# Later loads of the attention stacks, fewer transfers of x, and an earlier split of v's weights in a kernel of attention and a gated MLP

## The chip, the cores and the metric

The kernel runs on one core of a Trainium2 chip. A core has five engines that work side by side, each through its own list of instructions in order: TensorE (PE, matrix products; PEld is its loading of weights), VectorE (DVE), ScalarE (ACT), GpSimd (POOL) and SyncE (SP), which here only issues transfers. Sixteen DMA engines move data between the chip's large memory (DRAM) and the core's on-chip memory. The metric is the device time of one execution in microseconds (us). The kernel before took 2613.21 us (median of three executions, 2612.97 to 2613.29).

## The reference

`x` has 2048 tokens of 576 features; attention has 32 heads of 18 features, the MLP 4608 hidden units. All is fp32.

```python
xn = _layernorm(x)                                   # over the 576 features, eps 1e-5
q, k, v = split(xn @ wqkv)                           # 32 heads x 18
p  = softmax(einsum("bhqd,bhkd->bhqk", q, k) * 18 ** -0.5)
s  = (p @ v) @ wo
h  = (xn @ w_gate) * (xn @ w_up)                     # 576 -> 4608
g  = silu(h @ w_down)                                # 4608 -> 576
return x + s * g
```

## The kernel before, in words

**Numbers in two parts.** TensorE multiplies in a reduced form of fp32. An operand that must keep its precision is therefore held as two parts, a high one (a copy by ACT that rounds) and a low one (the difference, by DVE or POOL). A product is then three matmuls: high by high, low by high, high by low.

**Three stages.** In the *prologue* (0 to 197 us of the trace) x is normalised, turned so that features lie on partitions, and multiplied by the weights of q, k and v, chunk by chunk; a chunk is 512 tokens and there are four. q and k are stored, in their two parts, to the DRAM array `sqk` (lines 440 to 455), v to `sv` (`v_block`), the turned x to `sx`. The *main stage* (197 to about 2530 us) does attention's scores and the MLP mixed with each other. In the *epilogue* (to 2610 us) attention's output is multiplied by `wo` and everything is joined.

**The prologue's place.** v's weights come in two halves of 288 columns. `v_split(h)` splits half `h` into parts: five pieces, each an ACT copy (L493) and a POOL difference (L494), into `wv`. `v_block` multiplies the x of 128 tokens by `wv` (L502), first half 0, then half 1. In the loop over chunks `c` and blocks `b`, the step `norm` starts the layernorm of chunk `c + 2`; its ACT part is a tiny square root, `rs` (L344), that waits for statistics of DVE.

**The main stage's two array halves.** TensorE's array is used as two halves, each with 64 rows: partitions 0 to 63 (r = 0) and 64 to 127 (r = 1). Half 0 does the first look at each head's scores: 64 *a items*, each a matmul 128 queries x 512 keys (L648) whose maximum DVE takes (L650). When a head is through, its maxima are folded (L656), negated and split (L662, L666), turned and written by SP as two more rows (`mr`, L686) under the head's q. Half 1 does the same scores again, transposed and with the maximum subtracted by these rows: 64 *b items* (L700), each followed by ACT's exponential (L702) into `pt`. The *visits* multiply `pt` by v (L711); there are three for a head, of 6, 5 and 5 tiles of keys, before the change and after it.

The MLP's units run between the items: for each of 18 units of a chunk, 27 matmuls for up on half 0 and 27 for gate on half 1 (L753), then down (L804). At a unit's gate end the hidden value is `us` times the gate (L766), and its high part is made by ACT (`hs`, L771), its low part by POOL (`hs`, L784, in `low_now`). Down's results are summed into `acc` by DVE (L867) or by ACT and POOL. Weights of the MLP are split in chunk 0, kept in DRAM, and read back in the later chunks, one 1152 KB transfer for a unit's gate or up (`wgu`, L244) and one for its down (`wd`, L283).

**The stacks.** Both kinds of items read q and k from two tiles. Each holds in 18-row bands the high or low part of one head, so that the three products come out of one matmul. A head's *whole* tile is loaded in three transfers of 18 rows x 2048 tokens (144 KB each), its *turning* tile in two halves, part 0 and part 1, of three transfers of 18 x 1024 each (72 KB each). Both come from `sqk` by `load_stack` (L314 to L319), on SP. There are two whole tiles (they alternate by head) and one turning tile for each half of the array, whose halves are written over while the head runs. `stack_turn(r, h, i, h0)` is called at each item `i` of head `h` and says from which item a load may go (`at`: its old contents have been read) and at which item it must go (`by`):

```python
for at, by, g, part in ((0, 48, h + 1, None), (32, 48, h + 1, 0), (0, 16, h, 1)):
```

From `at` on, the load waits in the list `stacks`. Each gate end takes the first from it (`high`, L769 to L776); what is still there at item `by` is loaded at once.

**What sets the order.** A planner (`order()`) writes the instructions of the main stage while it simulates the engines with fixed costs: it keeps a clock for each half of the array (`clk`), times at which engines and banks come free, and for the transfers of SP one queue, at a rate of 0.24 MB per us:

```python
def moved(start, size):
    queue[0] = max(queue[0], start) + size / 0.24
    return queue[0] + 2.0
```

`moved(done - 0.4, 1.18)` books a weight load at each gate end (`done` is when the gate's last product has been taken), about 1.1 us ahead of the moment at which `high` runs. The planner lets a matmul of the MLP go only when its weights or its x are there by this booking (`loaded`, `downed`, `there`). On the chip SP works through its list in order.

**x for the next chunk.** At the last unit of a chunk, as soon as one of the nine blocks of x (64 features each, the high and the low part of 512 tokens) has been used for the last time, `x_block` loads the same block of the next chunk from `sx` over it, for each half its own copy: half 0 by SP, half 1 by POOL's own queue (L465 for block 4, which is in two parts, L468 for the others). A block is 64 partitions x 1024 numbers, 256 KB. In POOL's list these issues stand among its differences.

Of the kernel before, what the change touches and what calls it, by code (L numbers as in the profile page):

```python
# [20 lines left out]
FT = mybir.dt.float32  # L21
# [20 lines left out]
def kernel(  # L42
# [31 lines left out]
    sx = dram.tile([NCH, 9, 64, 2, 512], FT, name="sx")  # L74
# [101 lines left out]
    def engine(eng, start, length):  # L176
        start = max(free[eng], start)
        free[eng] = start + max(length - HIDDEN[eng], 0.03)
        return start + length
# [134 lines left out]
    def load_stack(r, h, part):  # L314
        tile, kind = (whole[h % 2], r == 0) if part is None else (turning, r != 0)
        cs = slice(0, S) if part is None else slice(part * S // 2, (part + 1) * S // 2)
        rows = slice(h * DH, (h + 1) * DH)
        for i, low in enumerate((0, 0, 1) if kind else (0, 1, 0)):
            nc.sync.dma_start(tile[r + i * DH:r + (i + 1) * DH, cs].bitcast(FT), sqk[int(kind), low, rows, cs])  # L319
# [120 lines left out]
    def qk_block(b, c):  # L440
        w, ninth = (t[:, b % 2] for t in wq[b // 2])
        p = bank("a" if nqk[0] % 2 else "b", 2)
        nqk[0] += 1
        for n, (a, e) in enumerate(QK_PAIRS):
            nc.tensor.matmul(p, w[:, a, :] if a < 9 else ninth, xcs[c][:, e, :], start=n == 0,  # L445
                             stop=n == len(QK_PAIRS) - 1)
        hl = pp.tile([128, 2, 512], FR, name="hl", bufs=3)
        nc.scalar.activation(hl[:, 0, :], p, AF.Copy)
        nc.vector.tensor_tensor(hl[:, 1, :], p, hl[:, 0, :].bitcast(FT), op=OP.subtract)
        g0 = blocks[b]  # L450
        for kind in range(2):
            lo, hi = max(g0, kind * D), min(g0 + 128, (kind + 1) * D)
            if lo < hi:
                dst = sqk[kind, :, lo - kind * D:hi - kind * D, c * 512:(c + 1) * 512]
                nc.sync.dma_start(dst.rearrange("h r s -> r h s"), hl[lo - g0:hi - g0].bitcast(FT))


    def x_part(b, part):
        return divmod(2 * b + part, 9)

    def x_block(c, b, r):
        queue = nc.gpsimd if r else nc.sync
        if b == 4:
            for part in range(2):
                queue.dma_start(xg[part][r:r + 64, 8 - 8 * part, :].bitcast(FT), sx[c, b, :, part, :])  # L465
        else:
            i, k = x_part(b, 0)
            queue.dma_start(xg[i][r:r + 64, k:k + 2, :].bitcast(FT), sx[c, b])  # L468

    vbox, vrows, vturn = {}, [], [0]  # L470

# [14 lines left out]
    def v_split(h):  # L486
        if h == 0:
            vbox["w"] = vp.tile([128, 10, D], FR, name="wv")
            more_rows(vp, 3)
        raw, wv = vbox["raw"], vbox["w"]  # L490
        cs = slice(h * HALF, (h + 1) * HALF)
        for k, d, lo in ((0, 0, 4), (1, 1, 5), (2, 2, 6), (3, 3, 7), (4, 8, 9)):
            nc.scalar.activation(wv[:, d, cs], raw[:, k, :], AF.Copy)  # L493
            nc.gpsimd.tensor_tensor(wv[:, lo, cs], raw[:, k, :], wv[:, d, cs].bitcast(FT),  # L494
                                    op=OP.subtract)
# [50 lines left out]
    for c in range(NCH):  # L546
        if c + 2 < NCH:
            load_x(c + 2)
        for b in range(3):
            qk_block(b, c)  # L550
            if c == 0 and b == 0:
                w_now(2)
        if c + 1 < NCH:
            to_columns(c + 1)
        for b in range(3, 6):
            qk_block(b, c)
            if b < 5 and c + 2 < NCH:
                norm(c + 2, (0, 1) if b == 3 else (2, 3))
            if c in (1, 2):
                x_store(c, range(3 * (b - 3), 3 * (b - 2)))  # L560
            if c < 2 and b == 3:
                v_split(c)
            if c == 0 and b == 5:
                v_fetch(1)
            if c == NCH - 1 and b == 3:
                w_now(3)
        if c == 1:
            w_fetch(3)
            for t in range(4):
                v_block(t)  # L570
            w_fetch(4)
        if c == 2:
            w_now(4)
# [56 lines left out]
    with ExitStack() as mid:  # L630
# [130 lines left out]
        def gate_end(n, ps):  # L761
            u, j = divmod(n, 2)
            if j == 0:
                hs[u] = mp.tile([128, 2, 2, 512], FR, name="hs", bufs=2)
            h32 = us.pop(n)
            nc.vector.tensor_tensor(h32, ps, h32, op=OP.mult)  # L766
            g_get(n + 2)
            hj = hs[u][:, j]

            def high(end):  # L770
                nc.scalar.activation(hj[:, 0, :], h32, AF.Copy)  # L771
                lows.append((n, hj, h32))
                pool_later.append((end + 0.1, 1.30, low_now))
                if stacks:
                    load_stack(*stacks.pop(0))
                    moved(end + 1.4, 0.88)  # L776

            return high

# [169 lines left out]
        def stream(r, kind):  # L949

            def glu(n):
                c, q = units[n // 2]
                box = []
                for k in range(len(TERMS)):
                    def work(k=k):
                        if k == 0:
                            box.append(gu_start(r, n))
                        gu_op(r, n, box[0], k)
                        if q == NF2 - 1 and n % 2 and k % 3 == 2 and c < NCH - 1:
                            x_block(c + 1, k // 3, 64 * r)  # L960
                            if r:
                                there["x", c + 1, k // 3, r] = engine("POOL", clk[r] + 0.5, 0.75 + 0.6 * (k == 14)) + 3.0
                            else:
                                there["x", c + 1, k // 3, r] = moved(clk[r] + 0.5, 0.285)
                        if n == 2 * len(units) - 1 and k == 13:
                            xdone.append(r)
                            if len(xdone) == 2:
                                wo_fetch()
                        if k == len(TERMS) - 1:
                            highs.append((gate_end if r else up_end)(n, box[0]))  # L970
                    end = (("DVE", 0.685) if r else ("ACT", 0.595)) if k == len(TERMS) - 1 else None
                    yield 0.231, k == 0, work, end, ("g", n, k), len(TERMS)

            def down(u, n):
                own = alone(u, n)
                key = u, n, r * own
                s, i = divmod(n, 2)
                for k in range(len(DTERMS)):
                    def work(k=k):
                        if (own or r == 0) and k == 0:  # L980
                            passed[key] = down_start(r, u)
                        down_op(r, u, s, i, passed[key], k, {"POOL": nc.gpsimd, "ACT": nc.scalar, "DVE": nc.vector}[soonest()])
                        if (own or r) and k == len(DTERMS) - 1:
                            acts.append(by_act(u, i, clk[r] + 0.33))
                            down_end(u, s, i, passed.pop(key), acts[-1])
                    end = None
                    if (own or r) and k == len(DTERMS) - 1:
                        end = (None, 0.0)
                    yield 0.132, (own or r == 0) and k == 0, work, end, ("d", u, 6 * n + k), len(DTERMS)

            if kind == "g":
                for n in range(2 * len(units)):
                    yield from glu(n)
            else:
                for u in range(len(units)):
                    for n in range(8):
                        yield from down(u, n)
# [19 lines left out]
# [4 lines that stand above are left out]
# [31 lines left out]

        def stack_turn(r, h, i, h0):

            for at, by, g, part in ((0, 48, h + 1, None), (32, 48, h + 1, 0), (0, 16, h, 1)):
                if not (g < H and (g > h0 if part is None else g > 0)):
                    continue
                if i == at:
                    stacks.append((r, g, part))
                if i == by and (r, g, part) in stacks:  # L1060
                    stacks.remove((r, g, part))
                    load_stack(r, g, part)
# [381 lines left out]
```

## Time and profile before

| what | us |
|---|---|
| median of three executions | 2613.21 |
| the profiled execution | 2611.95 |
| its span (first to last instruction) | 2610.2 |
| TensorE busy | 2595.7 (99%) |
| VectorE busy | 1795.3 (69%) |
| ScalarE busy | 1564.0 (60%) |
| GpSimd busy | 691.1 (26%) |

A row of a timeline is: start, length, engine, line, operation, output <- input, tile, count, and in brackets the idle time just before and what ended it. Some rows join several instructions (`x25`). A row of the list of waits is: engine, tile and line of the waiting instruction, what it waited for, us in total, times, longest. A row of the windows is: from:to, length, the busy time (and number) of PE, PEld, DVE, ACT and POOL, TensorE's granted clock, the busy share of the DMA engines, and GB/s; for one line of the kernel, only the busy time of its engine. A row of a group gives the busy time in total, the mean in ns, and the idle time before with its causes. The page lists transfers with their size and, where it can be told, the median time from issue to landing.

### The profile page before, as it was taken

To read this page: it belongs to the slowest core of one execution; us is meant where nothing else is said; L and a number is where in the kernel's file an instruction comes from. 1 tells how busy PE (TensorE), PEld (TensorE's weight loads), DVE (VectorE), ACT (ScalarE), POOL (GpSimd) and SP (SyncE) were. 2 spreads that over 40 slices of the span, in tenths; PEclk is the share of its full clock that TensorE was granted. 3 is DMA by queue.
4 is the path that set the end of the run, shared out by engine and by line. 5 is a ranking of instruction groups with operands and counts; after the bars stand their busy time and mean duration, and the time that the engine had idled before them with its cause. 6 is when DMAs were issued, how large, how long until landed. Compare 5 with 4: busy or idle time off the path is not lost.

```text
span 2610.2 us, 59616 instructions
## 1 busy us (share of the span) xinstructions
PE 2595.7 (99%) x24504; PEld 2130.0 (82%) x24504; DVE 1795.3 (69%) x2985; ACT 1564.0 (60%) x3119; POOL 691.1 (26%) x731
## 2 busy tenths in 40 slices
PE   8999999999999999999999999999999999999999
PEld 7899878777878877887778888778788778777789
DVE  7208677677777877777777777777777777777436
ACT  4223667676766666666656666666666566666742
POOL 3114545343421222222121222112121222112115
PEclk9999999999999999999999999999999999999999
DMA  7799767667573534554463445344564444343356
GB/s 239 236 293 260 205 189 207 177 194 198 173 189 114 167 129 144 175 159 149 144 174 124 139 158 151 121 135 137 146 174 130 142 142 148 128 136 109 110 200 214
DMA packets 206928, 434.34 MB, mean 166 GB/s; under 512 B 82976, under 2 KB 132800, under 8 KB 176448
## 3 DMA queue, kind: packets, MB, share of 16 engines
q1 hardware_dynamic: 202288, 415.48, 52.6%
q0 software_dynamic: 4368, 15.04, 2.0%
q8 instruction: 193, 3.16, 0.5%
q14 instruction: 79, 0.65, 0.1%
HBM read 314.64 MB, written 110.56 MB: 163 GB/s over the span
## 4 chain that ended last, share of the span: by engine, by line
PE 96%; DMA 2%; DVE 1%; SPq 1%; ACT 0%; issue 0%; POOL 0%; ACTq 0%; DVEq 0%
PE pg L753 35%; PE pg L711 17%; PE pg L804 16%; PE pa L648 11%; PE pb L700 9%; PE pg L1396 2%; PE pg L502 1%; PE pb L445 1%; PE pa L445 1%; DMA sqk<-hl 1%; SPq L534 1%; DVE st L342 0%; DMA draw<-in_B_w_down_dram 0%; DMA sv<-vo 0%; PE pb L1373 0%; DVE mx L650 0%
## 5 line engine op out<-in xcount | busy, mean ns | idle before, releaser
L650 DVE TENSOR_REDUCE mx<-pa 128x1 f32<-128x512 f32 x2016 | 1345.6, 686 | 318.8 <-PE pa L648 182.7
L702 ACT ACTIVATE pt<-pb 128x512 f32<-128x512 f32 x2004 | 1148.7, 601 | 525.8 <-PE pb L700 384.8
L753 PE MATMUL pg<-xc,wgu 64*128 64x512 f32 x7776 | 1391.9, 391 | 0.1
L753 PEld LDWEIGHTS pg<-xc,wgu 64*128 64x128 f32 x7776 | 1053.7, 186 | 55.9 <-issue 0.8
L804 PE MATMUL pg<-wd,hs 64*128 64x288 f32 x6816 | 827.0, 293 | 0.7 <-DVE acc L867 0.7
L804 PEld LDWEIGHTS pg<-wd,hs 64*128 64x128 f32 x6816 | 773.9, 185 | 11.8 <-DVE acc L867 0.9
L648 PE MATMUL pa<-whole,turning 54*128 54x512 f32 x1999 | 783.5, 398 | 0.0
L700 PE MATMUL pb<-whole,turning 56*128 56x512 f32 x1987 | 778.5, 399 | 0.0
L711 PE MATMUL pg<-pt,vt 128*32 128x512 f32 x4096 | 459.3, 594 | 0.9 <-DVE acc L867 0.8
L784 POOL TENSOR_TENSOR hs<-us,hs 128x512 fp32r<-128x512 f32 x144 | 186.2, 1293 | 894.7 <-ACT hs L771 718.0
L648 PEld LDWEIGHTS pa<-whole,turning 54*128 54x128 f32 x1999 | 363.8, 184 | 71.8 <-issue 60.5
L700 PEld LDWEIGHTS pb<-whole,turning 56*128 56x128 f32 x1987 | 361.3, 185 | 7.0
L831 POOL TENSOR_TENSOR acc<-acc,st 128x288 f32<-128x288 f32 x288 | 231.7, 808 | 505.2 <-ACT st L861 289.4
L711 PEld LDWEIGHTS pg<-pt,vt 128*32 128x32 f32 x4096 | 123.3, 110 | 277.3 <-issue 269.0
L717 DVE TENSOR_TENSOR oc<-oc,pg 128x512 f32<-128x512 f32 x64 | 44.0, 687 | 287.9 <-PE pg L711 287.9
L254 POOL TENSOR_TENSOR wgu<-wraw,wgu 128x384 fp32r<-128x384 f32 x108 | 108.0, 1016 | 194.8 <-ACT wgu L253 108.8
L861 ACT ACTIVATE st<-pg 128x288 f32<-128x288 f32 x288 | 118.8, 413 | 31.3 <-PE pg L804 21.3
L867 DVE TENSOR_TENSOR acc<-acc,pg 128x288 f32<-128x288 f32 x257 | 114.6, 448 | 29.5 <-PE pg L804 24.1
L766 DVE TENSOR_TENSOR us<-pg,us 128x512 f32<-128x512 f32 x144 | 98.5, 684 | 31.4 <-PE pg L753 26.3
L759 ACT ACTIVATE us<-pg 128x512 f32<-128x512 f32 x144 | 86.2, 599 | 38.9 <-PE pg L753 31.3
L771 ACT ACTIVATE hs<-us 128x512 fp32r<-128x512 f32 x144 | 90.8, 631 | 10.6 <-DVE us L766 10.3
L715 ACT ACTIVATE oc<-pg 128x512 f32<-128x512 f32 x32 | 19.1, 598 | 127.6 <-PE pg L711 127.6
(147 smaller groups left out, 1290.7 us busy)
## 6 DMA issues: line engine op xcount, KB each, us to landing
wgu<-swg SPq DMA_DIRECT2D x102, 1152.0 KB
wd<-swd SPq DMA_DIRECT2D x50, 1152.0 KB
swg<-wgu SPq DMA_DIRECT2D x36, 1152.0 KB
whole<-sqk SPq DMA_DIRECT2D x192, 144.0 KB
turning<-sqk SPq DMA_DIRECT2D x384, 72.0 KB
swd<-wd SPq DMA_DIRECT2D x18, 1152.0 KB
sqk<-hl SPq DMA_DIRECT2D x32, 512.0 KB
wraw<-in_B_w_up_dram SPq DMA_DIRECT2D x36, 288.0 KB
```

The costliest lines, as they stand in the source:

```text
L254: nc.gpsimd.tensor_tensor(w[:, 9 + b:12 + b, :], raw[:, b:b + 3, :], w[:, b:b + 3, :].bitcast(FT), op=OP.subtract)
L648: nc.tensor.matmul(p, q[rows, t * 128:(t + 1) * 128], k[rows, c * 512:(c + 1) * 512], start=True, stop=True)
L650: nc.vector.tensor_reduce(mx[h][:, t, c:c + 1], p, axis=AX.X, op=OP.max)
L700: nc.tensor.matmul(p, k[rows, t * 128:(t + 1) * 128], q[rows, c * 512:(c + 1) * 512], start=True, stop=True)
L702: nc.scalar.activation(pt[t, c // 2][:, c % 2, :], p, AF.Exp, scale=scale)
L711: nc.tensor.matmul(p[32 * c:32 * c + 32, :], vt[h // 2][:, t, 6 * (h % 2):6 * (h % 2) + 32], pt[t, c // 2][:, c % 2, :], start=t == ts[0], ...
L753: nc.tensor.matmul(ps, gw[n][half[r], a, :], xg[i][half[r], e, :], start=k == 0, stop=k == len(TERMS) - 1)
L784: nc.gpsimd.tensor_tensor(hj[:, 1, :], h32, hj[:, 0, :].bitcast(FT), op=OP.subtract)
L804: op = nc.tensor.matmul(ps[:, 0:HALF], hs[u][half[r], j, a, s * 128:(s + 1) * 128], dw[u][half[r], j, e, i * HALF:(i + 1) * HALF], start=( ...
L831: nc.gpsimd.tensor_tensor(a, a, st, op=OP.add)
L861: nc.scalar.activation(st, ps[:, 0:HALF], AF.Copy)
L867: nc.vector.tensor_tensor(a, a, ps[:, 0:HALF], op=OP.add)
```

## The change

There are three parts.

First, `v_split(1)` is called before `norm` and `x_store` instead of after them (chunk 1, block 3). ACT at this place (`hl` and `vo` are the stored parts of q, k and v), before:

```order
L448 ACTIVATE hl<-pa 128x512
L344 ACTIVATE rs<-mv,eps 128x1 x2
L493 ACTIVATE wv<-wvraw 128x288 x5
L448 ACTIVATE hl<-pb 128x512
L344 ACTIVATE rs<-mv,eps 128x1 x2
```

and after:

```order
L448 ACTIVATE hl<-pa 128x512
L497 ACTIVATE wv<-wvraw 128x288 x5
L344 ACTIVATE rs<-mv,eps 128x1 x2
L448 ACTIVATE hl<-pb 128x512
L344 ACTIVATE rs<-mv,eps 128x1 x2
```

The five copies have moved past the first two square roots; nothing else of ACT's list moves.

Second, half 1's x comes in eight transfers at each chunk change instead of ten: blocks 5 and 6, and 7 and 8, are joined, and go when the second of a pair has been used. The planner books half 1's x on SP's planned queue as well. POOL at the first chunk change (`xc` is x's tile), before:

```order
L468 DMA xc<-sx 64x1024 x3
L784 TENSOR_TENSOR hs<-us,hs 128x512
L468 DMA xc<-sx 64x1024
L465 DMA xc<-sx 64x512 x2
L468 DMA xc<-sx 64x1024 x4
L784 TENSOR_TENSOR hs<-us,hs 128x512
```

and after:

```order
L468 DMA xc<-sx 64x1024 x3
L791 TENSOR_TENSOR hs<-us,hs 128x512
L468 DMA xc<-sx 64x1024
L465 DMA xc<-sx 64x512 x2
L471 DMA xc<-sx 64x2x1024 x2
L791 TENSOR_TENSOR hs<-us,hs 128x512
```

Four issues ahead of the second difference have become two.

Third, a gate end takes a stack load from the list only when the planned queue has run down to `end + 1.0`, and the items at which loads must go are 52 and 20 instead of 48 and 16. SP at about 1805 us of the trace (`wgu` and `wd` are weights, `mr` the rows of the maxima), before:

```order
L319 DMA whole_1154<-sqk 18x2048 x3
L244 DMA wgu<-swg 128x2304
L319 DMA whole_1153<-sqk 18x2048 x3
L319 DMA turning<-sqk 18x1024 x6
L283 DMA wd<-swd 128x2304
L244 DMA wgu<-swg 128x2304 x2
L319 DMA turning<-sqk 18x1024 x3
L686 DMA whole_1153<-mr 1x16x128 x2
```

and after:

```order
L283 DMA wd<-swd 128x2304
L244 DMA wgu<-swg 128x2304
L319 DMA whole_1154<-sqk 18x2048 x3
L319 DMA turning<-sqk 18x1024 x3
L244 DMA wgu<-swg 128x2304
L692 DMA whole_1153<-mr 1x16x128 x2
```

The load of `whole_1154` for the next head stood ahead of `wd` (the `wd` that the trace shows at 1805.09 us) and now stands behind it and a `wgu`, directly followed by the turning tile's part 0. Over the whole program a whole load is followed directly by a turning load at 61 places instead of 24, and SP's list has 684 rows instead of 699.

TensorE's and VectorE's lists are the same before and after, instruction by instruction, except for line numbers. The diff:

```diff
@@ x_block
         if b == 4:
             for part in range(2):
                 queue.dma_start(xg[part][r:r + 64, 8 - 8 * part, :].bitcast(FT), sx[c, b, :, part, :])
-        else:
+        elif b < 5 or not r:
             i, k = x_part(b, 0)
             queue.dma_start(xg[i][r:r + 64, k:k + 2, :].bitcast(FT), sx[c, b])
+        elif b in (6, 8):
+            i, k = x_part(b - 1, 0)
+            queue.dma_start(xg[i][r:r + 64, k:k + 4, :].rearrange("p (b e) s -> p b e s", b=2).bitcast(FT),
+                            sx[c, b - 1:b + 1].rearrange("b p e s -> p b e s"))
@@ the prologue's loop
             qk_block(b, c)
+            if c == 1 and b == 3:
+                v_split(c)
             if b < 5 and c + 2 < NCH:
                 norm(c + 2, (0, 1) if b == 3 else (2, 3))
             if c in (1, 2):
                 x_store(c, range(3 * (b - 3), 3 * (b - 2)))
-            if c < 2 and b == 3:
+            if c == 0 and b == 3:
                 v_split(c)
@@ high, in gate_end
-                if stacks:
-                    load_stack(*stacks.pop(0))
-                    moved(end + 1.4, 0.88)
+                if stacks and queue[0] <= end + 1.0:
+                    part = stacks.pop(0)
+                    load_stack(*part)
+                    moved(end + 1.4, 0.44 if part[2] is None else 0.22)
@@ stream, at the last unit of a chunk
-                            x_block(c + 1, k // 3, 64 * r)
-                            if r:
-                                there["x", c + 1, k // 3, r] = engine("POOL", clk[r] + 0.5, 0.75 + 0.6 * (k == 14)) + 3.0
-                            else:
-                                there["x", c + 1, k // 3, r] = moved(clk[r] + 0.5, 0.285)
+                            b = k // 3
+                            x_block(c + 1, b, 64 * r)
+                            if not r or b not in (5, 7):
+                                pair = r and b in (6, 8)
+                                at = moved(clk[r] + 0.5, 0.57 if pair else 0.285)
+                                if r:
+                                    at = max(at, engine("POOL", clk[r] + 0.5, 0.75 + 0.6 * (b == 4)) + 2.0)
+                                for e in (b - 1, b) if pair else (b,):
+                                    there["x", c + 1, e, r] = at
@@ stack_turn
-            for at, by, g, part in ((0, 48, h + 1, None), (32, 48, h + 1, 0), (0, 16, h, 1)):
+            for at, by, g, part in ((0, 52, h + 1, None), (32, 52, h + 1, 0), (0, 20, h, 1)):
```

## The prediction

> **What bounds the kernel now.** I read the page's first lines, its chain, and its transfers.
>
> ```profile
> span 2610.2 us, 59616 instructions
> PE 2595.7 (99%) x24504; PEld 2130.0 (82%) x24504; DVE 1795.3 (69%) x2985; ACT 1564.0 (60%) x3119; POOL 691.1 (26%) x731
> ...
> PE 96%; DMA 2%; DVE 1%; SPq 1%; ACT 0%; issue 0%; POOL 0%; ACTq 0%; DVEq 0%
> ...
> wgu<-swg SPq DMA_DIRECT2D x102, 1152.0 KB
> wd<-swd SPq DMA_DIRECT2D x50, 1152.0 KB
> ...
> whole<-sqk SPq DMA_DIRECT2D x192, 144.0 KB
> turning<-sqk SPq DMA_DIRECT2D x384, 72.0 KB
> ```
>
> TensorE is busy for 99% of the span and carries 96% of the chain. Its instructions are the same 9718 rows in the same order before and after, so the change can only remove waits of TensorE or add some. How much there is to remove, the view of waits tells: TensorE's own list, complete.
>
> ```profile
> PE pg L404 <- DVE xn L353: 6.5, 2, 6.2
> PE pg L502 <- POOL wv L494: 1.0, 3, 0.4
> PE pg L711 <- DVE acc L867: 0.8, 2, 0.7
> PE pg L804 <- DVE acc L867: 0.7, 1, 0.7
> PE pa L679 <- DVE neg L666: 0.6, 1, 0.6
> PE pb L445 <- ACT xcx L406: 0.5, 1, 0.5
> ```
>
> No row names a transfer: no load of stack parts, weights or x ends later than TensorE wants it. The stack loads can therefore give nothing; moving them later can only cost. The rows that the change can touch are L502 (v's weights) and the two of `acc` L867, if they are connected with x.
>
> **Part 1: v's second weights split sooner.** The timeline of the prologue from 53 us, ACT first, then POOL and TensorE:
>
> ```profile
> 53.61 0.60 ACT L448 ACTIVATE hl<-pa 128x512 fp32r<-128x512 f32 x1 [3.73 <-DMA sqk<-hl]
> 55.94 0.29 ACT L344 ACTIVATE rs<-mv,eps 128x1 f32<-128x1 f32 x1 [1.73 <-DVE mv L343]
> ...
> 57.06 1.76 ACT L493 ACTIVATE wv<-wvraw 128x288 fp32r<-128x288 f32 x5
> ...
> 57.57 4.05 POOL L494 TENSOR_TENSOR wv<-wvraw,wv 128x288 fp32r<-128x288 f32 x5 [18.62 <-ACT wv L493]
> ...
> 56.26 3.61 PE L502 MATMUL pg<-wv,xcx 128*128 128x288 f32 x25
> 60.17 0.40 PE L502 MATMUL pg<-wv,xcx 128*128 128x288 f32 x1 [0.30 <-POOL wv L494]
> 60.92 0.40 PE L502 MATMUL pg<-wv,xcx 128*128 128x288 f32 x1 [0.35 <-POOL wv L494]
> 61.67 11.53 PE L502 MATMUL pg<-wv,xcx 128*128 128x288 f32 x85 [0.35 <-POOL wv L494]
> ```
>
> The first v block takes POOL's low parts one by one as they come. At 25 matmuls in 3.61 us, 0.144 each, the two that stand alone stretch the way from 59.87 to 61.67 to 1.80 us where two matmuls want 0.29: 1.5 us lost (at least 1.0 by the list of waits). In the changed order the five activations `wv` stand in front of the two norm activations `rs`, so they start at 54.2 (53.61 + 0.60), where ACT is idle for 1.73 us now, instead of 57.06: 2.85 us sooner. POOL follows, being free since long (18.62 us idle), and ends near 58.8 instead of 61.6. All three waits go: −1.5 us, between −1.0 and −1.5. What could eat it: `rs` is held until 54.2 + 1.76 = 55.97 against 55.94 now, 0.03 us. From 62 to 197 us TensorE's list shows no further wait, so the gain is passed on whole.
>
> **Part 2: half 1's x in eight transfers.** At each of three chunk changes POOL issues eight instead of ten transfers. The group of all L468 issues, and the first chunk change:
>
> ```profile
> L468 POOL DMA_DIRECT2D xc<-sx x24 | 12.6, 524 | 46.3 <-PE pg L753 22.7 <-PE pa L648 20.5 <-PE pb L700 2.2
> ...
> 738.34 0.51 POOL L468 DMA_DIRECT2D xc<-sx  x1 [1.82 <-PE pb L700]
> 738.86 1.29 POOL L784 TENSOR_TENSOR hs<-us,hs 128x512 fp32r<-128x512 f32 x1
> ...
> 737.84 0.62 ACT L771 ACTIVATE hs<-us 128x512 fp32r<-128x512 f32 x1
> ...
> 738.98 1.22 DVE L666 SCALAR_TENSOR_TENSOR neg<-m,neg 128x16 fp32r<-128x16 f32 x1
> ...
> 740.62 0.79 PE L804 MATMUL pg<-wd,hs 64*128 64x288 f32 x7 [0.67 <-DVE acc L867]
> 741.58 2.35 PE L711 MATMUL pg<-pt,vt 128*32 128x512 f32 x20 [0.17 <-DVE acc L867]
> ...
> L666 DVE SCALAR_TENSOR_TENSOR neg<-m,neg 128x16 fp32r<-128x16 f32 x32 | 10.7, 333 | 0.5 <-ACT neg L662 0.5
> ```
>
> Six issues fewer are 6 × 0.524 = 3.1 us of POOL, which is busy for 26% of the span: hidden. But the last issue at 738.34 holds POOL until 738.86, and the subtraction L784, whose input `hs` ACT has ready at 737.84 + 0.62 = 738.46, starts 0.40 us late. It then lies on DVE's L666, which takes 1.22 us here against a mean of 333 ns; the sum L867 behind it comes late, and TensorE waits 0.67 and 0.17 us. With L784 0.40 us sooner the collision ends 0.40 us sooner: −0.4 us, between 0 and −0.84 (both waits gone). [...] The joined transfers let block 7 of x land with block 8; TensorE took block 8 last before, so I price this at 0, at most +0.5 (one issue).
>
> **Part 3: stack parts later, and joined.** After a gate's end the new planner asks for a queue of at most `end + 1.0`, but the weight load booked just before puts it some 4.5 us ahead (1.18 MB at 0.24 MB/us). So the gate's end loads almost nothing any more, and parts go when forced: six transfers together at item 52 of 64, three at item 20. SP works its list in order; what counts is whether the six land before the next head's first item when a weight load or two stand ahead of them. Pace, the three tightest kinds of place, and what the next head needs:
>
> ```profile
> 738.00:1817.00 1079.00, 3.40 (x16) 1.00 0.47 147
> ...
> 826.00:838.00 12.00, 12.00 (x126) 11.99 (x123) 10.37 (x18) 10.45 (x20) 2.59 (x2) 1.00 0.82 276
> 1805.00:1813.00 8.00, 8.00 (x73) 7.86 (x72) 6.98 (x12) 6.54 (x13) 2.36 (x3) 1.00 0.76 297
> 1118.00:1124.00 6.00, 6.00 (x54) 6.00 (x53) 5.17 (x9) 4.70 (x9) 1.30 (x1) 1.00 0.73 247
> ...
> 826.13 0.35 SPq L283 DMA_DIRECT2D wd<-swd  x1
> 838.01 0.39 PE L700 MATMUL pb<-whole,turning 56*128 56x512 f32 x1
> 1805.09 0.34 SPq L283 DMA_DIRECT2D wd<-swd  x1
> 1816.12 0.39 PE L648 MATMUL pa<-whole,turning 54*128 54x512 f32 x1
> 1117.96 0.34 SPq L244 DMA_DIRECT2D wgu<-swg  x1
> 1128.41 0.40 PE L700 MATMUL pb<-whole,turning 56*128 56x512 f32 x1
> ...
> sg<-sil POOLq DMA_DIRECT2D x12, 288.0 KB, 2.9
> ```
>
> The first row is DVE's fold at a head's end, L656: 16 of them at both ends of 1079 us, so 15 heads of 71.9 us, 1.12 us an item. Item 52 leaves 12 items, 13.5 us, before the next head. In the windows the last figure is GB/s.
>
> A landing I estimate as the first heavy load's issue, plus bytes by the window's rate, plus a fixed 1.8 us: the 288 KB (0.295 MB) of `sg` land in 2.9 us, less 0.295 / 0.276 = 1.1. Six parts are 3 × 144 + 3 × 72 = 648 KB.
> - Behind `wd` and `wgu` (2304 + 648 = 2952 KB, 3.02 MB): 826.13 + 11.0 + 1.8 = 838.9, wanted at 838.01: 0.9 us late. And 1805.09 + 10.2 + 1.8 = 1817.1, wanted at 1816.12: 1.0 late. I count two places of this kind in the new order.
> - Behind one weight load (1800 KB, 1.84 MB): 1117.96 + 7.5 + 1.8 = 1127.3, wanted at 1128.41: 1.1 us early. A dozen places are of this kind (the new order of SP laid on the times of the trace), with 9.4 to 11.4 us between load and need; the estimate's own error is about a microsecond, so I book a sixth of one each: 2.0 us.
>
> Sum +3.9 us. Below, the bound is 0 (all in time; no gain, since no transfer is waited for). Above, the dozen late like the pair, 12 × 0.9 = 10.8. I take the value nearest to the rows: the pair as computed, the dozen nearly in time.
>
> [...]
>
> The `mr` rows, v's loads and the weights themselves stand elsewhere on SP, but each moves behind at most one joined load, six issues at about 0.35 us (the issue of `wd` at 826.13), 2.1 us, and none of them is waited for now: 0.
>
> **Sum.** −1.5 − 0.4 + 3.9 = +2.0 us. The profiled execution took 2611.95 us (span 2610.2 and 1.75 around it), so 2614.0 for an execution like it; the median of the runs shown lies 1.26 above that, 2613.21, and the forecast for the median is 2615.2.
>
> **Rivals.**
> - All parts land in time. For it: no transfer is late now, and over the 1079 us of fifteen heads the DMA engines are busy for 0.47. Against it: the pair's 0.9 us. Then 2613.2 − 1.5 − 0.4 = 2611.3. [...]
> - The other side: the joined parts are late at all fourteen tight places, 0.8 us on average, because they stand behind a full in-order SP queue at 826-like rates. 11 us, 2613.2 + 10.8 − 1.9 = 2622. It decides (slower by over 0.2%) from 7.1 us on, 0.5 us each at fourteen places, that is when the dozen land 1.6 us later than the estimate. For it: with 0.73 to 0.82 busy, the DMA engines are near full while such loads run. Against it: the 1.1 us of margin at 1118.
> - Stack parts no longer in the way of other transfers, so that weights come sooner and more than the two waits go. A gain over 5.2 us has no row: all waits of TensorE behind the prologue together are 2.1 us.
>
> **How the numbers follow.** 0.2%, 5.2 us, is about what a measurement of this kernel can tell from no change. The forecast of +2 us has 0.50, all in time 0.27, late at all places 0.18, a gain without a row 0.05. Faster is below 2608.0: 0.05; slower above 2618.4: the third case, 0.18; the rest, 0.77, is within. The range: below, all gains at their larger bounds and nothing late, 2613.2 − 2.3 = 2610.9, rounded to 2610.5; above, toward the rival, 2621, which leaves out the upper half of it.
>
> **What the profile after would show.** Part 1: no wait of L502's matmuls for `wv`. Part 2: 24 POOL issues of x, and L666 near 737 us back toward 0.33 us or colliding earlier. Part 3: new waits of the score matmuls (`whole,turning`) for `whole<-sqk` or `turning<-sqk` at heads' starts, first at 838 and 1816. The prediction is wrong if those waits add up to over 7 us, if some other load behind the joined parts (`wgu`, `wd`, x) becomes a wait, or if a wait at a chunk change grows because `hs` and L666 meet in another way.

## The result

The changed kernel takes 2626.43 us (median of six executions, 2623.28 to 2631.66) where the kernel before takes 2612.59 (2611.52 to 2613.29): a ratio of 1.0056, 95% interval 1.0043 to 1.0069. It is 13.8 us slower, 11.2 us above the forecast, and outside the range. The profiled execution is the slowest of the six, 2631.66 us; its sizes below are therefore some 5 us too large in sum, their kinds are not.

The page of the changed kernel: span, busy time, and the chain by engine, where DMA has grown from 2% to 4%.

```profile
span 2629.9 us, 59639 instructions
PE 2603.9 (99%) x24504; PEld 2133.9 (81%) x24504; DVE 1797.9 (68%) x2985; ACT 1565.1 (60%) x3119; POOL 688.3 (26%) x725
...
PE 94%; DMA 4%; SPq 1%; DVE 0%; issue 0%; ACT 0%; POOL 0%
```

TensorE's waits, complete. Two rows name the stack parts, 12.6 us in nine waits; the three waits for `wv` and the two for `acc` at the first chunk change are gone (the 0.7 us left for `acc` is at another place).

```profile
PE pa L654 <- DMA turning<-sqk: 8.5, 5, 3.1
PE pg L404 <- DVE xn L353: 6.6, 2, 6.3
PE pb L706 <- DMA turning<-sqk: 4.1, 4, 2.2
PE pb L706 <- ACT st L868: 0.9, 1, 0.9
PE pg L717 <- DVE acc L874: 0.7, 1, 0.7
PE pa L685 <- DVE neg L672: 0.6, 1, 0.6
PE pb L445 <- ACT xcx L406: 0.5, 1, 0.5
```

TensorE's list is the same in both kernels, so each matmul of the one trace can be laid on its counterpart in the other. The difference of their starts shows where time goes. These are the places at which it changes (start before, start after, difference, all in us, and the line in the kernel before). Just ahead of v's second weights the difference is +0.82, from the first 16 us, which the change doesn't touch; the first row is thus 1.70 us gained:

```
   61.67    60.79   -0.88  L502   v's second weights
  409.40   408.59   -0.82  L700
  479.75   479.96    0.21  L700   head's first item
  594.83   596.80    1.97  L648   head's first item
  692.97   697.46    4.49  L700   head's first item
  696.05   702.07    6.03  L711   the 3 us behind it
  740.62   746.14    5.52  L804   first chunk change
  837.92   844.29    6.37  L700   head's first item
 1173.71  1180.85    7.14  L648   head's first item
 1314.43  1322.72    8.29  L648   head's first item
 1816.06  1827.56   11.51  L648   head's first item
 1819.15  1832.23   13.08  L711   the 3 us behind it
 1922.19  1938.14   15.95  L648   head's turning tile, part 1
 1923.72  1941.05   17.33  L804   the 1.5 us behind it
 2124.45  2142.57   18.13  L700   head's first item
 2462.07  2481.40   19.33  L700   head's first item
```

Ten steps at first uses of a stack part (each against the matmul just ahead of it in the trace) add up to 16.4 us. Another 4.5 us comes right behind three of them (692.97, 1816 and 1922), and there the granted clock is down. The windows around 1824 us, with the clock in the third column from the end:

```profile
1816.00:1824.00 8.00, 8.00 (x84) 7.95 (x83) 7.24 (x11) 6.70 (x13) 1.17 (x2) 1.00 0.87 314
1824.00:1828.00 4.00, 0.88 (x12) 0.66 (x10) 0.91 (x2) 1.01 (x3) 0.80 (x1) 1.00 0.90 303
1828.00:1832.00 4.00, 4.00 (x34) 2.74 (x34) 2.53 (x5) 1.90 (x4) 1.60 (x2) 0.59 0.03 14
```

And the timeline of the places that the prediction had worked out, SP's issues and the item that waited:

```profile
831.34 0.35 SPq L283 DMA_DIRECT2D wd<-swd  x1
...
844.29 0.47 PE L706 MATMUL pb<-whole,turning 56*128 56x512 f32 x1 [0.91 <-ACT st L868]
...
1813.27 0.34 SPq L283 DMA_DIRECT2D wd<-swd  x1
...
1827.56 0.47 PE L654 MATMUL pa<-whole,turning 54*128 54x512 f32 x1 [3.12 <-DMA turning<-sqk]
...
1168.07 0.34 SPq L244 DMA_DIRECT2D wgu<-swg  x1
...
1180.85 0.46 PE L654 MATMUL pa<-whole,turning 54*128 54x512 f32 x1 [0.58 <-DMA turning<-sqk]
...
1311.74 0.34 SPq L283 DMA_DIRECT2D wd<-swd  x1
...
1322.72 0.46 PE L654 MATMUL pa<-whole,turning 54*128 54x512 f32 x1 [0.76 <-DMA turning<-sqk]
```

The first of these is put down to ACT, but the last of its stack parts lands at 843.98 by the trace's semaphore events, after that operation of ACT has ended (843.83), so it too is a wait for the transfer. From the first heavy load's issue to the item: 12.95 us and 14.29 behind `wd` and `wgu`, 12.78 and 10.98 behind one weight load.

### The profile page after: what moved, and what is told of

Read it like the earlier page. It is cut to its first block, busy times and chain, and to the rows that moved or that the text cites. A ratio compares the mean times of both kernels' runs of the same rounds, so it can differ in the third digit from the quotient of the medians.

```text
span 2629.9 us, 59639 instructions
## 1 busy us (share of the span) xinstructions
PE 2603.9 (99%) x24504; PEld 2133.9 (81%) x24504; DVE 1797.9 (68%) x2985; ACT 1565.1 (60%) x3119; POOL 688.3 (26%) x725
## 4 chain that ended last, share of the span: by engine, by line
PE 94%; DMA 4%; SPq 1%; DVE 0%; issue 0%; ACT 0%; POOL 0%
PE pg L759 33%; PE pg L717 17%; PE pg L811 15%; PE pa L654 10%; PE pb L706 8%; DMA turning<-sqk 3%; PE pg L1407 2%; PE pb L445 2%; PE pa L445 2%; PE pg L506 2%; SPq L538 1%; SPq L319 0%; DMA so<-ot 0%; PE pb L1384 0%; DMA xc<-sx 0%
```

## The experiments

**The parts apart.** The first kernel (e1) undoes part three; the split sooner and x in eight transfers stay:

```diff
-                if stacks and queue[0] <= end + 1.0:
-                    part = stacks.pop(0)
-                    load_stack(*part)
-                    moved(end + 1.4, 0.44 if part[2] is None else 0.22)
+                if stacks:
+                    load_stack(*stacks.pop(0))
+                    moved(end + 1.4, 0.88)
...
-            for at, by, g, part in ((0, 52, h + 1, None), (32, 52, h + 1, 0), (0, 20, h, 1)):
+            for at, by, g, part in ((0, 48, h + 1, None), (32, 48, h + 1, 0), (0, 16, h, 1)):
```

> Parts one and two of the change without the third: v's second weights split sooner and half 1's x in eight transfers, while the stack parts are loaded as before. Theory (the whole loss is stack parts that land after the first item that needs them): no wait of TensorE for a stack part, 2612.6 - 1.5 - 1.0 = 2610.1 us. Rival (the joined transfers of x crowd out the stack parts at the chunk changes, where the changed kernel lost 2.9 us and then 1.5 us at about 1922 us): that loss stays, 2610.1 + 4.4 = 2614.5 us.

Measured: 2614.38 us (11 runs, 2610.91 to 2616.19) against 2611.84 for the kernel before, ratio 1.0010 (1.0001 to 1.0019). The size is the rival's, 2.5 us slower than before and not 1.7 faster, but its mechanism is not to be seen: in the profile, which is of the fastest execution, TensorE waits for no stack part. Something of part one or two costs by itself. The opposite kernel (e2) has part three alone (the same lines, put into the kernel before):

> Part three alone: stack parts at a gate's end only when the planned queue has run down, and forced at items 52 and 20; the split and x as before. Theory: all of the loss and none of the gains, 2.5 us above the changed kernel, 2626.4 + 2.5 = 2628.9 us. Rival (x in eight transfers takes part in the loss at about 1922 us): 2628.9 - 4.4 = 2624.5 us.

Measured: 2631.3 us (5 runs, 2629.07 to 2635.81), ratio 1.0078 (1.0065 to 1.0091). The loss is part three's, 19.5 us by itself, more even than the whole change costs. Its profile (span 18.6 us longer), laid on the kernel before, has 10.0 us of this at first uses of stack parts and 3.0 behind two stalls, where the clock is down; 2.1 more come at the first chunk change, from POOL (below), and 0.9 in the prologue, which part three doesn't touch.

**Condition or items.** Two kernels take the two halves of part three apart. In the first (e3) the items go back to 48 and 16 and the condition stays; in the second (e4) the old rule at a gate's end comes back and the items stay at 52 and 20 (each is one of the two pieces of the diff above).

> The changed kernel with the items at which stack loads are forced put back to 48 and 16; the condition on the planned queue stays, so that nearly all parts still go when forced, joined, but four items (4.5 us) sooner. Theory (it is the lateness alone, at most 3.3 us in the changed kernel's profile): no wait for a stack part is left, 2610.1 us, and after no stall does the granted clock fall. Rival (the joined loads are late because they queue behind weights wherever they are put): half of the loss or more stays, 2618 us or above.

> The changed kernel with the old rule at a gate's end (the first part in the list is loaded there, whatever the queue); the forced items stay 52 and 20. Theory: nearly all parts go at gate ends as before, before they are forced, so the later items hardly matter: 2610 to 2613 us. Rival (the later items alone are enough for the loss): 2620 us or above.

Measured: 2612.4 us (11 runs; ratio 1.0005, 0.9996 to 1.0014) and 2611.8 us (11 runs; ratio 1.0002, 0.9993 to 1.0011). Either half alone costs next to nothing. With the old rule the parts go at gate ends, long before they are forced; with items 48 and 16 they are forced and joined, but 4.5 us sooner, and that is enough nearly everywhere. Not quite: the profile of the second has one wait of 1.2 us at a head's turning tile, for which it names no cause, and the profiled execution of the first (2619.08 us, the slowest of its 11) has one wait for a stack part, at the head's first item at 594.83:

```profile
PE pa L654 <- DMA turning<-sqk: 2.9, 1, 2.9
```

**How it goes with lateness.** The changed kernel with the items two later still (e8):

```diff
-            for at, by, g, part in ((0, 52, h + 1, None), (32, 52, h + 1, 0), (0, 20, h, 1)):
+            for at, by, g, part in ((0, 54, h + 1, None), (32, 54, h + 1, 0), (0, 22, h, 1)):
```

> The changed kernel with stack loads forced two items (2.25 us) later still, at 54 and 22. In the changed kernel's profile 22 of 122 first uses have less than 2.25 us between the landing of their part and themselves, and the shortfalls add up to 33 us beyond the waits that are there. Theory A (each late part costs its lateness): 2626 + 33 = 2659 us. Theory B (a stall of more than some 2.3 us also costs the fall of the granted clock behind it, about 1.6 us in the changed kernel's profile): a dozen more such falls, 2659 + 14..19 = 2673 to 2678 us, and a mean clock under 0.995. Rival (the loss does not go with the lateness of the parts): under 2635 us.

Measured: 2679.17 us (2 runs, 2675.89 and 2682.45), ratio 1.0256. That is theory B, 1 us above the end of its range. The profile's two rows of waits, its mean clock, and the window behind the longest stall, which ends at 415.69:

```profile
PE pb L706 <- DMA turning<-sqk: 25.7, 12, 6.1
PE pa L654 <- DMA turning<-sqk: 22.8, 8, 5.2
```

```profile
core 0: 2680.7 us, clock 0.991
```

```profile
416.00:420.00 4.00, 4.00 (x23) 1.61 (x25) 0.69 (x1) 0.60 (x1) 0.00 (x0) 0.50 1.02 286
```

The waits come to 48.5 us; the span has grown by 70.5. Laid on the kernel before, some 56 us lie at first uses (more than the waits, which count only time without any matmul), and 17 us right behind nine of these stalls, where the clock is down.

**Why late.** Two kernels try to say why the parts take so long. One (e9) issues the stack loads from ACT's own queue:

```diff
-            nc.sync.dma_start(tile[r + i * DH:r + (i + 1) * DH, cs].bitcast(FT), sqk[int(kind), low, rows, cs])
+            nc.scalar.dma_start(tile[r + i * DH:r + (i + 1) * DH, cs].bitcast(FT), sqk[int(kind), low, rows, cs])
```

> The changed kernel with the stack loads issued by ACT on its own queue, at the same places of the program, in place of SP. Theory A (the parts are late because they stand behind one or two weight loads of 1152 KB in SP's queue): they land some 5 us sooner, the waits for them go, 2610 to 2615 us. Theory B (the narrow transfers of 18 partitions, about 1.0 us for 144 KB where 1152 KB of weights take 3.0 us, are slow in themselves, whatever stands ahead): half of the loss or more stays, 2619 us or above. Either way, ACT pays for nine issues a head.

Measured: 2782.05 us (4 runs), ratio 1.0646. It decides nothing between the two, because a third thing took over: ACT's exponentials now stand behind its own issues, which wait for earlier transfers to land (73.5 us, 36 times), and TensorE waits for the exponentials.

```profile
PE pb L706 <- ACT pt L708: 98.5, 58, 11.0
...
PE pa L654 <- DMA turning<-sqk: 1.6, 1, 1.6
PE pb L706 <- DMA turning<-sqk: 0.8, 1, 0.8
```

```profile
ACT pt L708 <- DMA turning<-sqk: 73.5, 36, 11.7
```

The other (e11) sends the same bytes from the same place in smaller transfers:

```diff
-            nc.sync.dma_start(tile[r + i * DH:r + (i + 1) * DH, cs].bitcast(FT), sqk[int(kind), low, rows, cs])
+            for c0 in range(cs.start, cs.stop, S // 2):
+                cc = slice(c0, c0 + S // 2)
+                nc.sync.dma_start(tile[r + i * DH:r + (i + 1) * DH, cc].bitcast(FT), sqk[int(kind), low, rows, cc])
```

> The changed kernel with each transfer of 18 x 2048 (144 KB) issued as two of 18 x 1024 (72 KB): the same bytes in the same place of SP's list, three issues more for a head. By the order of landings in the changed kernel's trace a band of 144 KB takes about 1.0 us behind its forerunner, one of 72 KB 0.4. Theory (the shape of the narrow transfers makes up the lateness): a whole tile lands some 0.6 us sooner, less 1.0 us for three more issues where SP itself is behind, so 0 to 0.6 us at each of a dozen places, 2619 to 2626 us. Rival (only the weights ahead count, or the limit of transfers under way holds the longer list back): as the changed kernel or slower, 2626 to 2640 us.

Measured: 2625.75 us (6 runs, 2623.95 to 2636.18), ratio 1.0059 (1.0045 to 1.0072): as the changed kernel. The length of a band in one transfer is not what makes the parts late.

The trace of the changed kernel says more. Behind the load issued at 831.34, first weights alone move and then stack parts alone, by the sizes of the packets in the trace. A window of each:

```profile
834.00:838.00 4.00, 4.00 (x38) 4.00 (x36) 3.48 (x6) 2.83 (x5) 0.30 (x1) 1.00 1.01 429
839.50:841.50 2.00, 2.00 (x29) 2.00 (x27) 1.64 (x3) 1.68 (x4) 0.00 (x0) 1.00 0.55 133
```

The parts move at a third of the weights' rate, 133 GB/s instead of 429 (behind 1813.27 it is 143 instead of 438), and the DMA engines are then only 0.55 busy. By the semaphore events a weight load lands in sixteen steps and a part in nine. So both of e9's theories have a part in it: at 831.34 the weights ahead take 8.0 us, until 839.35 by the semaphore events, and the parts behind them 4.6, for a fifth of the bytes. Whether it is the 18 rows that make them slow was not shown: no kernel here loads more rows at a time.

**The split and x.** The split alone (e5) is the prologue's piece of the diff, put into the kernel before; x alone (e6) is its pieces in `x_block` and `stream`.

> The kernel before with v's second weights split sooner, and nothing else. Theory (TensorE's three waits for the split go, and nothing follows): 2611.9 - 1.5 = 2610.4 us. Rival (the split that moves ahead of the norm's square roots delays the prologue elsewhere, which is why e1 was not faster): 2612 us or above.

> The kernel before with half 1's x in eight transfers, and nothing else. Theory, formed after e1 (the pair of blocks 7 and 8 lands as one at the last chunk change, 0.04 us before block 7 is needed in e1's fastest execution, so in others later): e1 plus the split's gain, 2614.4 + 1.5 = 2615.9 us. Rival (x costs nothing, the loss of e1 is the split's): 2611 to 2612 us.

Measured: the split alone 2610.57 us (11 runs) against 2611.87, ratio 0.9994 (0.9985 to 1.0002), 1.3 us less, as forecast in size though not clear of the noise. x alone 2613.93 us (11 runs, 2612.34 to 2616.09), ratio 1.0008 (0.9999 to 1.0017), 2.1 us more: less than the theory's 4, but with the place that it named. Of x alone: TensorE's wait, its place, the issues of POOL at the last change, and the time from issue to landing of the joined transfers (min, median, max); below them POOL's issues there in the kernel before.

```profile
PE pg L757 <- DMA xc<-sx: 2.1, 1, 2.1
...
1935.74 1.20 PE L757 MATMUL pg<-xc,wgu 64*128 64x512 f32 x8 [2.14 <-DMA xc<-sx]
...
1916.89 0.60 POOL L471 DMA_DIRECT2D xc<-sx  x1 [6.03 <-PE pg L757]
1918.91 0.60 POOL L471 DMA_DIRECT2D xc<-sx  x1 [1.43 <-PE pa L652]
...
DMA to landing us min/median/max: 11.5/13.7/16.8
```

```profile
1910.85 0.52 POOL L468 DMA_DIRECT2D xc<-sx  x1 [0.37 <-PE pa L648]
...
1917.83 0.52 POOL L468 DMA_DIRECT2D xc<-sx  x1 [5.16 <-PE pg L753]
1918.52 0.52 POOL L468 DMA_DIRECT2D xc<-sx  x1 [0.16 <-PE pg L804]
1919.84 0.51 POOL L468 DMA_DIRECT2D xc<-sx  x1 [0.80 <-PE pa L648]
```

Block 5 used to leave at 1910.85; joined with block 6 it waits until 1916.89. The last pair, issued at 1918.91, takes 16.8 us, until 1935.7, where in the kernel before, by the semaphore events of its trace, block 7 alone landed at 1929.82 and was wanted at 1934.21. To see whether that pair is all of it, the next kernel (e10) takes e1 and parts blocks 7 and 8 again at the last change only:

```diff
-        elif b < 5 or not r:
+        elif b < 5 or not r or c == 3 and b > 6:
```

> e1 (split and x, stack parts as before) with blocks 7 and 8 of half 1 again in two transfers, at the last chunk change only. Theory (the late pair there is all that e1 lost): 2611.9 - 1.5 - 0.9 = 2609.5 us. Rival (the loss of e1 lies at the other changes, or in the split): 2613 to 2614.4 us as e1.

Measured: 2611.91 us (11 runs), ratio 1.0001 (0.9992 to 1.0009). It gives back 2.5 us of e1's loss, half of the 4.9 that the theory asked for. Its profile shows the rest at the same change: block 8, though alone again, is waited for once, behind the pair 5 and 6, which still leaves late.

```profile
PE pg L759 <- DMA xc<-sx: 1.7, 1, 1.7
```

So the next one (e12) joins at the first change only and leaves the others as before (stack parts as before, split sooner; the condition above reads `c > 1`):

> The split sooner, the stack parts as before, and x of half 1 in eight transfers at the first chunk change only (ten at the other two). Theory (the joined transfers cost at the last change, where blocks 7 and 8 had 4.4 and 0.9 us to spare, and gain 0.9 us at the first, where POOL comes free sooner): 2611.9 - 1.3 - 0.9 = 2609.7 us. Rival (the first change's gain is in the profiles alone, or x costs there too): 2610.6 us, as the split alone, or more.

Measured: 2610.1 us (11 runs, 2609.49 to 2611.55) against 2611.67, ratio 0.9993 (0.9984 to 1.0001). It is the fastest kernel measured here, 1.6 us under the kernel before, though its interval still reaches 1. Each against the runs of before that it shares, it stands 0.3 us better than the split alone, where 0.9 was expected; such a difference is too small to be told. Its profile speaks for the rival: at the first change TensorE's two waits for `acc` are there as before.

**Why the parts don't add.** Apart they come to −1.3, +2.1 and +19.5, in sum +20.3; together to +13.8. In the profile of part three alone TensorE waits at the first chunk change for POOL, which executes a hand-over of a bank (L809) behind its ninth and tenth issue of x; the tenth waits for an earlier transfer to land:

```profile
746.45 0.51 POOL L468 DMA_DIRECT2D xc<-sx  x1 [4.09 <-PE pg L805]
748.88 0.51 POOL L468 DMA_DIRECT2D xc<-sx  x1 [1.92 <-DMA xc<-sx]
...
748.94 0.93 PE L805 MATMUL pg<-wd,hs 64*128 64x288 f32 x10 [2.48 <-POOLq L809]
```

The last kernel (e13) therefore is part three with x joined at the first change only:

> Part three with x of half 1 in eight transfers at the first chunk change only; ten at the others, the split as before. The parts alone came to 1.3 us less (split), 2.1 us more (x) and 19.5 us more (stacks), 20.3 in sum, where the whole change costs 13.8. Theory (the missing 6.5 us: with part three alone POOL waits at the first change with its ninth and tenth issue of x, and TensorE 2.5 us for a hand-over that POOL executes behind them, which the joined transfers remove, together with the 0.9 us that they gain there without part three): 2631.3 - 2.5 - 0.9 = 2627.9 us. Rival (the first change has no part in it): 2631 us, as part three alone.

Measured: 2627.97 us (5 runs, 2624.01 to 2634.79), ratio 1.0064 (1.0050 to 1.0078), as the theory had it, and its profile has no wait for the hand-over. But the two waits for `acc` at that place, 0.9 us in the theory, have not gone, so that the number agrees partly by luck; with executions that spread over 10 us this supports the place rather than proves its size. The other 3 us have a possible cause that was not tried apart: in the whole change, by the semaphore events of its trace, the last pair of x lands 6.15 us before it is wanted, because TensorE, held up by the stack parts just before, comes to it later; the 2.1 us that x costs alone cannot be lost there a second time.

## Why the prediction was wrong

- **The sign of part three was right, its mechanism at half of the places, its size not.** The prediction said that parts forced at items 52 and 20 would stand behind weight loads on SP and land after their first use, and booked 3.9 us. Alone it costs 19.5.
- **The step that failed is the count of the places: "I count two places of this kind" and "A dozen places are of this kind", all behind weight loads, with every other first use at nothing and no reason for it.** Of the ten late first uses, five are such others (479.75, 594.83, 692.97, 1922.19 and 2462.07), with 9.4 of the 16.4 us. In the first chunk SP also stores the split weights and fetches raw ones, and at 1922 us the parts share the queue with x. Ahead of three of the five the DMA engines are busy throughout; for 2462 no reason is known.

```profile
588.00:596.00 8.00, 7.32 (x64) 6.89 (x60) 6.65 (x11) 6.38 (x15) 2.78 (x3) 1.00 1.00 190
688.00:697.00 9.00, 7.25 (x62) 6.25 (x58) 7.23 (x11) 6.51 (x13) 3.47 (x4) 1.00 1.06 240
1926.00:1938.00 12.00, 9.56 (x100) 6.44 (x92) 5.74 (x10) 5.21 (x10) 2.46 (x3) 1.00 1.04 205
```

- **The term of the dozen came out near by luck.** It booked 2.0 us, a sixth of one at each place; the profile has 2.5, at three places (1173.71, 1314.43, 2124.45), and nothing at the others. By the semaphore events the six parts landed 9.7 to 12.6 us after the one weight load's issue, at 28 places, half of them within 9.94; the estimate was 9.3. It took the mean rate of a window in the kernel before (247 GB/s) for weights and parts alike; the two places at 1311 and 1168 us moved 1.84 MB at 200 and 168 GB/s (less 1.8 us).
- **The pair was half right.** At 838 us, 12.8 us were worked out and 12.95 measured, 0.9 us late and 1.15 lost. At 1816 us, 12.0 were worked out and 14.29 measured: 1.0 us late became 3.3 lost.
- **A term was missing: the clock behind a stall.** The prediction priced a wait at its length. In the changed kernel's profile three stalls of 2.2 to 3.1 us cost 1.4 to 1.6 us each on top, 4.5 in sum. With 9.4 at places without a figure, 2.6 more at the pair and 0.5 more at the dozen, that is the 17 us by which part three cost more than booked in this profile.
- **The split was right**: −1.5 forecast, −1.3 measured alone, and the waits for `wv` are gone. ACT's five copies run at once behind `hl`, and `rs` starts 2.33 us after `hl` does, as before (55.94 less 53.61). All ten profiles with the earlier split gain 1.70 us at this place. Of the three new ones without it two gain nothing; in that of x alone the waits are gone too, since ACT's copies start 0.9 us sooner there and TensorE comes 0.8 us later, so that the absence of the waits in one profile proves little by itself.

```profile
52.39 0.60 ACT L448 ACTIVATE hl<-pa 128x512 fp32r<-128x512 f32 x1 [3.84 <-DMA sqk<-hl]
52.89 1.77 ACT L497 ACTIVATE wv<-wvraw 128x288 fp32r<-128x288 f32 x5
54.72 0.29 ACT L344 ACTIVATE rs<-mv,eps 128x1 f32<-128x1 f32 x1
```

- **x gained nothing at the first change, and cost at the last.** At the first change −0.4 was forecast, on the ground that the last issue of x holds POOL's subtraction. In the two traces the difference of starts does fall by about 1.0, from 6.47 at 737.55 to 5.52 at 740.62; but not because of x. In x alone and in six more kernels with the pairs joined there (e1, e3, e4, e10, e12, e13) POOL is done with its last issue some 1.6 us before the subtraction starts, DVE's operation still takes 1.17 to 1.19 us, and both of TensorE's waits stay. In x alone the subtraction, with nothing of x ahead of it, waits for TensorE and starts 0.38 us behind ACT's result, where it was 0.40 before:

```profile
737.93 1.28 POOL L788 TENSOR_TENSOR hs<-us,hs 128x512 fp32r<-128x512 f32 x1 [1.64 <-PE pg L808]
...
738.07 1.17 DVE L670 SCALAR_TENSOR_TENSOR neg<-m,neg 128x16 fp32r<-128x16 f32 x1
...
739.66 0.78 PE L808 MATMUL pg<-wd,hs 64*128 64x288 f32 x7 [0.65 <-DVE acc L871]
```

In the changed kernel (the rows below) DVE's operation begins 0.10 us before POOL's and takes 0.17 us. Part three alone, with ten issues of x, has the 0.17 us as well. So the gain comes with part three's later items, though not in all kernels that have them (e13 lacks it), and why the two operations change places there stays open. At this place the VectorE operation takes 1.17 to 1.22 us in the traces where the GpSimd one began before it, and 0.17 us where it began first. At the last change the price was "0, at most +0.5", on the ground that block 8 had been taken last before. But a pair leaves only when its second block is free, and lands later than either block did; alone that costs 2.1 us.

```profile
745.13 0.17 DVE L672 SCALAR_TENSOR_TENSOR neg<-m,neg 128x16 fp32r<-128x16 f32 x1
...
745.23 1.29 POOL L791 TENSOR_TENSOR hs<-us,hs 128x512 fp32r<-128x512 f32 x1 [1.88 <-PE pg L811]
```

- **The rival on the other side came nearest**: late parts behind a full queue, at 2622 us and with a chance of 0.18. But of its fourteen places only five are late, with 1.4 us at each instead of 0.8; the other five late places are not its own. "Parts always in time" had 0.27 on the strength of a DMA share of 0.47; a mean over 1079 us says nothing of the 12 us behind two weight loads.

## What to carry to other kernels

Before a load is moved later in an in-order queue, work out its landing at every place, and not only behind the heaviest transfers, with a rate for each kind of transfer (429 and 133 GB/s here, for weights and stack parts); take the spread of such landings as its price. A margin of one microsecond that rests on a window's mean rate is no margin. When transfers are joined, the new one leaves when its last piece may be overwritten and is awaited by its first, so both margins have to be there. And price a stall of TensorE of two to three microseconds at more than its length: three of 2.21 to 3.12 us cost 1.4 to 1.6 us each on top here.

## What the runs showed of the hardware

The granted clock of TensorE fell to one half behind some stalls: 0.59 to 0.61 as the mean of the 4 us behind stalls of 3.12 and 2.21 us of the changed kernel, 0.50 behind the longest of e8, 6.1 us. The length of the stall alone doesn't decide: in the changed kernel the clock falls behind 2.21 us, in e8 it doesn't behind 2.35 (at 725.67), so the 2.3 us of e8's theory B is no threshold; and in e11 it falls behind a stall of 1.66 us and doesn't behind one of 2.87.

```profile
696.37 0.47 PE L708 MATMUL pb<-whole,turning 56*128 56x512 f32 x1 [1.66 <-DMA turning<-sqk]
...
697.00:701.00 4.00, 4.00 (x23) 2.32 (x23) 1.38 (x2) 2.07 (x4) 2.23 (x2) 0.57 0.89 341
...
1828.59 0.47 PE L656 MATMUL pa<-whole,turning 54*128 54x512 f32 x1 [2.87 <-DMA turning<-sqk]
...
1829.00:1833.00 4.00, 4.00 (x48) 2.35 (x48) 2.43 (x5) 1.90 (x4) 1.61 (x2) 1.00 0.38 158
```

In the trace's records of the clock, the changed kernel's three falls begin at 698.89, 1828.70 and 1937.93 us and last 3.41 us each. 3.41 us at half the clock lose up to 1.7, of which 1.4 to 1.6 were measured.
